# Reordering the first front and the second batch's front of an attention-plus-mixer kernel

## The chip, the core and the metric

The kernel runs on one core of a Trainium2 chip. The metric is the device time of one launch in microseconds (us), taken from several launches; the median of three runs of the kernel before is 269.89 us (269.8 to 270.16). Beside those runs there is one profiled execution of the same program, which carries a record of every instruction of the five engines: PE (TensorE, matmuls), DVE (VectorE), ACT (ScalarE), POOL (GpSimd) and SP (SyncE, which here only issues DMAs).

## The reference: what is computed

Inputs are q, k, v of shape (8 batches, 8 heads, 576 positions, 64) and four weight matrices. For each batch and head a linear attention with cosine weights is computed:

```
c, s   = cos, sin of (pi/2 * position / 576)
phi(x) = [relu(x)*c, relu(x)*s]                 64 -> 128 features
kv     = sum over positions of phi(k)^T v       128 x 64
z      = sum over positions of phi(k)           128
x      = phi(q) kv / (phi(q) z + 1e-6)          per head; heads side by side: 576 x 512
```

Then a mixer over tokens and one over channels follow, for each batch:

```
B  = relu(w_tok1^T x)          256 x 512
u  = x + w_tok2^T B            576 x 512
out = u + relu(u w_ch1) w_ch2  hidden width 1536
```

## The kernel before

A batch has 576 positions: four chunks of 128 (R = 4; chunks 0 to 3) and a tail of 64. The tails of two batches share one 128-row tile, the even batch in rows 0 to 63, the odd one in rows 64 to 127 (class `Tail`, L166). Everything that follows attention is matmul work in bf16 with results in PSUM.

Two classes carry the work of a batch. `Front` (L216) goes from q, k, v to u: `feature` (L246) makes phi of one chunk, one instruction for the cosine half and one for the sine half, on DVE or on ACT; `values` (L266) casts v; `kv` (L309) accumulates kv over the chunks, `kv_out` (L328) copies it to SBUF in two halves of four heads, half 0 on ACT and half 1 on DVE; `q_trans` (L335) transposes the eight heads of phi(q) on PE and copies them out with ACT; `num` (L353) multiplies phi(q) by kv and lets DVE divide; `tok1` (L373) and `tok1_out` (L385) make B, its first 128 rows' relu on ACT and the second 128 rows' on DVE; `tok2` (L391) makes u. `Channel` (L532) does the channel mixer: `c_main` (L540) makes one of the twelve 128-wide strips of the hidden layer (four matmuls of 512 columns, then a relu on ACT), `o_step` (L572) accumulates two of the twelve strips into a chunk of the output.

The order of the work is written out by hand, engine by engine: every engine runs its instructions in the order in which the program emits them. The main loop (L748) walks the `Channel` steps of batch b (step i makes strip i, or the next piece of the output) and after each step emits the pieces of the front of batch b+1 that `pieces` (L461) has planned for that slot. In `pieces` an entry such as `(5, KS, 2, True)` means: in slot 5, both k features of chunk 2, the sine one on ACT. QS is the same for q, QT a transpose, V a cast of v, KV the kv matmuls, N a `num`, u a `tok2` of the batch before.

Batch 0 has no earlier batch to hide behind. Its front is `first_front` (L636). It holds filler matmuls (`busy`, L202: 512-column products of the identity and zeros that nobody reads), twelve at its head and more between the pieces. It computes the denominators separately: `ksum` (L278) sums phi(k) with one-column matmuls, `ksum_out` (L291) copies the sums, `dens` (L295) multiplies phi(q) with them (eight one-column matmuls for each chunk) and `dens_out` (L305) adds 1e-6 and takes the reciprocal. The first u of batch 0 is needed transposed, as the input of the channel mixer: `turned_x` (L422) puts x transposed into four PSUM tiles (16 matmuls against the identity), `turned_b` (L430) adds the w_tok2 product to them (eight matmuls of 512 columns), and the copies at L707 write uT. The twelve matmuls of `c_block` (L552) use it at once. The u of batch 0 in its plain layout, which the output needs, is made later, in the slots of batch 1's front.

PSUM is cut into two pools of tiles: `ps_mm` (four buffers) and `ps_at` (two larger buffers). A matmul into a buffer waits until its former content has been read.

The loads: q, k, v come through SP (one through ACT). The weights w_ch1 (four DMAs, L188) and w_ch2 (L196) come through POOL, which casts them to bf16 on the way. w_ch2 is loaded in three thirds, in slot 8 of batch 1's front, on POOL's queue between two casts of v; the load of batch 2's k waits for the second third (L760). Batch 1's u is turned by DMA transposes that SP issues (`u_trans_dma`, L437) after ACT has cast u to bf16.

## Time and profile before

| what | before |
|---|---|
| median of the runs shown | 269.89 us (269.8 to 270.16) |
| time of the profiled execution | 269.69 us |
| its span, first to last instruction | 267.9 us |
| PE busy, share of the span | 261.1 us, 97% |
| DVE, ACT, POOL busy | 164.5, 129.6, 14.5 us |
| granted TensorE clock, mean | 1.000 |
| filler matmuls in the first front at L204, 512 columns | 12 at the head, 21 in all later ones |

The profiled execution is 0.20 us below the median of the runs. Its span leaves 1.79 us for what lies before the first and after the last instruction. In a timeline each row gives the start and the length of one merged group of instructions on an engine, its line, what it writes and reads and how often; a bracket at the end is the idle time of the engine just before and who ended it. Matmuls are pipelined: a row's length includes the drain of its last matmul, so the distance between the starts of neighbouring rows tells what a group took of PE's time.

### The profile page before, as it was taken

How to read it: one execution, taken by the hardware profiler on the slowest of the kernel's cores; microseconds unless marked ns; L12 is line 12 of the kernel's file. 1: busy time of each engine (PE TensorE's matmuls, PEld its weight loads, DVE VectorE, ACT ScalarE, POOL GpSimd, SP SyncE). 2: the span in 40 equal slices, each digit the busy share in tenths (PEclk: the TensorE clock that was granted, in tenths of full speed). 3: DMA queues.
4: the chain of work that ended last, by engine and by line, in shares of the span. 5: the costliest groups of instructions: out<-in, count | busy, mean ns of one | idle time of the engine just before them, and what ended most of it. 6: DMA issues, size and time to landing. Idle time of an engine off the chain costs nothing.

```text
span 267.9 us, 5123 instructions
## 1 busy us (share of the span) xinstructions
PE 261.1 (97%) x2050; PEld 139.5 (52%) x2050; DVE 164.5 (61%) x376; ACT 129.6 (48%) x228; POOL 14.5 (5%) x24
## 2 busy tenths in 40 slices
PE   7989999999999999999999999999999999999994
PEld 2665466455644455446644455446644455445543
DVE  5965798784566846876565846876565846820022
ACT  3982876428606362546516362547515362526400
POOL 6450230000000000000000000000000000000000
PEclk9999999999999999999999999999999999999999
DMA  7999999679999999469974999199974580170032
GB/s 222 359 232 270 350 175 274 225 198 290 166 340 282 273 176 346 124 166 273 209 265 117 289 223 348 59 183 239 238 253 117 157 120 0 57 200 1 2 109 87
DMA packets 91815, 53.68 MB, mean 200 GB/s; under 512 B 59408, under 2 KB 86928, under 8 KB 91792
## 3 DMA queue, kind: packets, MB, share of 16 engines
q1 hardware_dynamic: 88432, 49.62, 69.7%
q0 software_dynamic: 2832, 3.21, 7.6%
q10 hardware_dynamic: 528, 0.52, 0.6%
q8 instruction: 16, 0.26, 0.4%
q14 instruction: 7, 0.06, 0.1%
HBM read 35.85 MB, written 9.44 MB: 169 GB/s over the span
## 4 chain that ended last, share of the span: by engine, by line
PE 92%; DVE 3%; ACT 2%; DMA 2%; issue 0%; DVEq 0%; ACTq 0%
PE o_ps L579 35%; PE c_ps L546 29%; PE u_ps L406 6%; PE b_ps L382 6%; PE num_ps L359 4%; PE ct_ps L566 4%; PE kv_ps L320 3%; DMA qt<-in_q_dram 2%; DVE qp L263 1%; PE idle_ps L204 1%; PE qT_ps L340 1%; ACT v_aug L274 1%; PE c_ps L556 1%; ACT h1T L550 1%; PE t_ps L433 1%; PE d_ps L302 0%
## 5 line engine op out<-in xcount | busy, mean ns | idle before, releaser
L579 PE MATMUL o_ps<-w_ch,h1T 128*128 128x512 bf16 (+1 forms) x396 | 94.1, 372 | 0.0
L546 PE MATMUL c_ps<-uT,w_ch 128*128 128x512 bf16 (+2 forms) x384 | 92.2, 372 | 0.1
L550 ACT ACTIVATE h1T<-c_ps 128x512 bf16<-128x512 f32 x93 | 55.4, 598 | 59.9 <-PE c_ps L546 59.5
L579 PEld LDWEIGHTS <-h1T 128*128 128x128 bf16 x396 | 37.3, 98 | 39.5 <-issue 0.2
L546 PEld LDWEIGHTS <-w_ch 128*128 128x128 bf16 x384 | 33.5, 97 | 29.6 <-issue 0.2
L584 DVE TENSOR_TENSOR o_sb<-o_ps,u_sb 128x512 f32<-128x512 f32 (+1 forms) x33 | 22.3, 674 | 29.5 <-PE o_ps L579 29.4
L409 DVE TENSOR_TENSOR u_sb<-u_ps,x_sb 128x512 f32<-128x512 f32 x32 | 21.7, 689 | 6.0 <-PE u_ps L406 5.6
L413 ACT CAST u_bf<-u_sb 128x512 bf16<-128x512 f32 x28 | 17.3, 619 | 16.7 <-DVE u_sb L409 16.7
L406 PE MATMUL u_ps<-B,w_tok 128*128 128x512 bf16 x80 | 22.6, 379 | 0.0
L387 ACT ACTIVATE B<-b_ps 128x512 bf16<-128x512 f32 x8 | 4.8, 597 | 35.4 <-PE b_ps L382 35.4
L369 DVE TENSOR_TENSOR x_sb<-num_ps,den 128x512 bf16<-128x512 f32 x28 | 19.4, 692 | 1.0
L566 PEld LDWEIGHTS <-w_ch 128*128 128x128 bf16 x192 | 14.0, 98 | 9.2
L382 PE MATMUL b_ps<-x_sb,w_tok 128*128 128x512 bf16 x64 | 17.9, 379 | 0.0
L566 PE MATMUL ct_ps<-uT_tail,w_ch 128*128 128x128 bf16 x192 | 17.2, 219 | 0.0
L263 DVE TENSOR_SCALAR kp<-kt,cos_t 128x512 bf16<-128x512 f32 x32 | 15.1, 478 | 3.1 <-DMA kt<-in_k_dram 3.1
L274 ACT CAST v_aug<-vt 128x512 bf16<-128x512 f32 (+1 forms) x30 | 16.7, 586 | 0.1
L263 DVE TENSOR_SCALAR qp<-qt,cos_t 128x512 bf16<-128x512 f32 (+1 forms) x35 | 15.9, 453 | 1.0 <-DMA qt<-in_q_dram 1.0
L263 DVE TENSOR_SCALAR qp<-qt,sin_t 128x512 bf16<-128x512 f32 (+1 forms) x35 | 15.9, 453 | 0.0
L584 DVE TENSOR_TENSOR o_sb<-o_ps,u_tail 128x512 f32<-128x512 f32 x4 | 2.8, 692 | 19.0 <-PE o_ps L579 19.0
L359 PEld LDWEIGHTS <-qpT 128*128 128x128 bf16 x256 | 11.5, 98 | 5.5 <-issue 1.3
L359 PE MATMUL num_ps<-kv_sb,qpT 128*128 128x65 bf16 x256 | 13.0, 193 | 0.9 <-DVE x_sb L369 0.5
L331 DVE CAST kv_sb<-kv_ps 128x260 bf16<-128x260 f32 x8 | 3.5, 433 | 16.6 <-ACT kv_sb L331 16.5
(93 smaller groups left out, 233.4 us busy)
## 6 DMA issues: line engine op xcount, KB each, us to landing
out_dram<-o_sb SPq DMA_DIRECT2D x31, 256.0 KB, 2.9
kt<-in_k_dram SPq DMA_DIRECT2D x7, 1024.0 KB, 6.7
vt<-in_v_dram SPq DMA_DIRECT2D x7, 1024.0 KB, 6.5
qt<-in_q_dram SPq DMA_DIRECT2D x7, 1024.0 KB, 8.3
w_ch<-in_moe_w_ch_dram POOLq DMA_DIRECT2D x4, 384.0 KB, 8.3
w_ch<-in_moe_w_ch_dram POOLq DMA_DIRECT2D x3, 512.0 KB, 7.5
out_dram<-o_sb SPq DMA_DIRECT2D x10, 128.0 KB, 2.3
qtt<-in_q_dram SPq DMA_DIRECT2D x8, 128.0 KB, 5.6
```

Source lines behind the costliest of these rows:

```text
L263: nc.vector.tensor_scalar(o_ap, i_ap, scalar1=w, scalar2=0.0, op0=ALU.mult, op1=ALU.max)
L274: nc.scalar.copy(dst, src)
L359: nc.tensor.matmul(num_ps[:, g, j * DP:j * DP + D1], self.qT_of(ci, h), self.kv_sb[g][:, j, 0:D1], start=True, stop=True)
L369: nc.vector.tensor_mul(self.x_of(ci)[rows].rearrange("p (g j d) -> p g j d", g=2, j=HH), nv[:, :, :, 0:D], den.to_broadcast([rows.stop - r ...
L382: nc.tensor.matmul(self.b1_ps[mi], w, self.x_of(ci), start=(ci == ORDER[0]), stop=(ci == ORDER[-1]))
L406: nc.tensor.matmul(u_ps, w_tok2[:, ki, ci * P:(ci + 1) * P], self.B1[:, ki, :], start=(ki == 0), stop=(ki == NT - 1))
L409: nc.vector.tensor_add(u, u_ps[rows], self.x_of(ci)[rows])
L546: nc.tensor.matmul(c_ps[:, lo:hi], w_ch1[:, ki, mi * P:(mi + 1) * P], uT[:, lo // P:hi // P, ki, :], start=(ki == 0), stop=(ki == NCC - 1))
L550: nc.scalar.activation(self.h1T[:, mi, :], c_ps, AF.Relu)
L566: nc.tensor.matmul(self.ct_ps[:, mi % R, :], w_ch1[:, ki, mi * P:(mi + 1) * P], self.tail.uT[:, ki, :], start=(mi % R == 0 and ki == 0), s ...
L579: nc.tensor.matmul(o_ps, h, w_ch2[:, ki, cols], start=ki == 0, stop=ki == NCH - 1)
L584: nc.vector.tensor_add(o_sb, o_ps, u)
```

## The change

It touches the first front, the tail's transposes, the plan of batch 1's front, the order of batch 0's output steps and the load of w_ch2.

- The tail's q features are transposed by a new function, `q_trans_last`: only the batch's own 64 rows are transposed (64 columns for each head instead of 128), and ACT copies only their half of the transposed tile. The other half of that tile is set to zero once at the start by POOL, in place of half of the `qp` tail tile. It is used for batch 0 and batch 1.
- In the first front the k features are emitted first and the one-column sums behind them, with fillers of 4 (before the features) and then 2, 2, 2, 1, 0; before, there were 2, then 2 in front of each of the five sums and one behind. The v cast of chunk 0 now stands ahead of `ksum_out` on ACT and the other three behind it. All five chunks' `dens` and one `dens_out` come before the first `kv`; the two casts of w_tok1 come behind both `kv_out`s.
- Six of the sixteen `turned_x` matmuls (chunks 0 to 2 of the first two tiles) are emitted between the tail's and the last chunk's `tok1`. B's relu is made in two halves of 256 columns on each engine.
- In batch 1's front u of batch 0 is emitted in slots 4, 5, 6, 7, 8 (before: 5, 6, 8, 9, 10), the tail's v cast moves from slot 7 to 9, the q features of chunk 0 from 9 to 10, and those of chunk 2 from DVE in slot 11 to ACT in slot 10, both halves.
- w_ch2 comes in four DMAs (strips 0-1, 2-3, 4-7, 8-11) in place of three of four strips each. Batch 0's output steps alternate between chunks 0 and 1 after every two strips instead of every four. Batch 2's k waits for the third of the four DMAs, which ends with the same strip as the second third did.

```diff
@@ -177,8 +177,8 @@
             self.uT = once.tile([P, NCC, P], BF16, name="uT_tail")
     tail0 = Tail(0)
-    for t in (tail0.kp, tail0.qp):
-        nc.gpsimd.memset(t[half(1)], 0.0)
+    nc.gpsimd.memset(tail0.kp[half(1)], 0.0)
+    nc.gpsimd.memset(tail0.qpT[:, :, half(1)], 0.0)
     for g in range(2):
         nc.gpsimd.dma_start(out=w_tail1[half(g), :], in_=moe_w_tok1[SM:S, :])
     C2 = D_ch // 2
@@ -191,11 +191,10 @@
                 .rearrange("(n c) d -> c n d", c=P)))
     after(w_ch1_done[0], k_done)
     w_ch2_done = []
-    def load_w_ch2(third):
-        ki = third * NCH // 3
+    def load_w_ch2(k0, k1):
         w_ch2_done.append(nc.gpsimd.dma_start(
-            out=w_ch2[:, ki:ki + 4, :],
-            in_=moe_w_ch2[ki * P:(ki + 4) * P, :].rearrange("(n t) d -> t n d", t=P)))
+            out=w_ch2[:, k0:k1, :],
+            in_=moe_w_ch2[k0 * P:k1 * P, :].rearrange("(n t) d -> t n d", t=P)))
@@ -345,6 +344,15 @@
             else:
                 nc.vector.tensor_copy(dst, qT_ps)
+        def q_trans_last(self, pool=ps_mm):
+
+            qT_ps = pool.tile([P, H, ST], BF16, name="qT_ps", tag="mm" if pool is ps_mm else "at")
+            for h in range(H):
+                nc.tensor.transpose(qT_ps[:, h, :],
+                                    self.tail.qp[self.rows, h, :, :].rearrange("p a b -> p (a b)"),
+                                    ident[self.rows, self.rows])
+            nc.scalar.copy(self.tail.qpT[:, :, self.rows], qT_ps)
+
         def q_trans_dma(self, ci):
             dst = self.qpT[:, ci * H:(ci + 1) * H, :] if ci < R else self.tail.qpT
             nc.sync.dma_start_transpose(out=dst,
@@ -382,11 +390,11 @@
                 nc.tensor.matmul(self.b1_ps[mi], w, self.x_of(ci),
                                  start=(ci == ORDER[0]), stop=(ci == ORDER[-1]))
-        def tok1_out(self, mi, on_act=True):
+        def tok1_out(self, mi, on_act=True, cols=slice(0, Dm)):
             if on_act:
-                nc.scalar.activation(self.B1[:, mi, :], self.b1_ps[mi], AF.Relu)
-            else:
-                nc.vector.tensor_relu(self.B1[:, mi, :], self.b1_ps[mi])
+                nc.scalar.activation(self.B1[:, mi, cols], self.b1_ps[mi][:, cols], AF.Relu)
+            else:
+                nc.vector.tensor_relu(self.B1[:, mi, cols], self.b1_ps[mi][:, cols])
         def tok2(self, ci, pool=None, turn=True):
             res, tail = self.res, self.tail
@@ -419,13 +427,12 @@
             self.res["uT"] = keep.tile([P, R * NCC, P], BF16, name="uT")
-        def turned_x(self, dst, kb, first):
-
-            for ci in range(R):
+        def turned_x(self, dst, kb, chunks=range(R)):
+
+            for ci in chunks:
                 nc.tensor.matmul(dst[:, ci * P:(ci + 1) * P],
-                                 self.x[:, ci, kb * P:(kb + 1) * P], ident, start=first,
+                                 self.x[:, ci, kb * P:(kb + 1) * P], ident, start=(ci == 0),
                                  stop=False, skip_group_check=True)
-                first = False
         def turned_b(self, dst, kb, cols):
@@ -446,8 +453,8 @@
             self.feature("k", ci, 0)
             self.feature("k", ci, 1, on_act=on_act)
-        def q_side(self, ci, on_act=False):
-            self.feature("q", ci, 0)
+        def q_side(self, ci, on_act=False, both=False):
+            self.feature("q", ci, 0, on_act=both)
             self.feature("q", ci, 1, on_act=on_act)
         def mix_head(self, mi):
@@ -469,16 +476,17 @@
             if first:
                 u, act, pool = before.tok2, nc.scalar, nc.gpsimd
-                plan = [(4, KS, 0), (4, KS, 1), (5, u, 0, ps_at, False), (5, KS, 2, True),
-                        (6, KS, 3, True), (6, u, 1, ps_at, False), (7, KS, R), (7, V, R, nc.vector), (8, V, 0, act),
-                        (8, V, 2, pool), (8, load_w_ch2, 0), (8, V, 3, pool),
-                        (8, load_w_ch2, 1), (8, load_w_ch2, 2),
-                        (8, u, 2, None, False), (9, V, 1, act), (9, u, 3, None, False),
-                        (9, QS, 0), (10, u, R, None, False)]
+                plan = [(4, u, 0, ps_at, False), (4, KS, 0), (5, u, 1, ps_at, False),
+                        (5, KS, 1), (5, KS, 2, True), (6, u, 2, None, False), (6, KS, 3, True),
+                        (7, u, 3, None, False), (7, KS, R), (8, u, R, None, False),
+                        (8, V, 0, act), (8, V, 2, pool), (8, load_w_ch2, 0, 2), (8, V, 3, pool),
+                        (8, load_w_ch2, 2, 4), (8, load_w_ch2, 4, 8), (8, load_w_ch2, 8, NCH),
+                        (9, V, R, nc.vector), (9, V, 1, act),
+                        (10, QS, 0), (10, QS, 2, True, True)]
                 plan += [(11, KV, ci) for ci in range(NSC)]
-                plan += [(11, QS, 1), (11, QS, 2), (11, self.kv_out),
+                plan += [(11, QS, 1), (11, self.kv_out),
                          (11, QT, 0, (0, H), act, ps_at), (11, QT, 1), (11, QS, R),
-                         (O, QT, 2), (O, N, 0), (O, QS, 3), (O + 1, QT, R),
+                         (O, QT, 2), (O, N, 0), (O, QS, 3), (O + 1, self.q_trans_last),
                          (O + 1, N, 1), (O + 3, N, 2), (O + 3, QT, 3),
                          (O + 5, N, R), (O + 7, N, 3), (O + 8, before.tail_cast)]
             else:
@@ -616,9 +624,9 @@
             if self.b == 0:
-                for lo in range(0, NCH, 4):
+                for lo in range(0, NCH, 2):
                     for ci in (0, 1):
-                        o_range(ci, lo, lo + 4)
+                        o_range(ci, lo, lo + 2)
                 rest = (2, 3)
             elif self.b == B - 1:
                 rest = (R, 0, 1, 2)
@@ -650,37 +658,33 @@
                 f.q_trans(ci, heads)
                 busy(idle_ps, 1)
         f.q_side(R)
-        f.q_trans(R, pool=ps_at)
-        busy(idle_ps, 2)
+        f.q_trans_last(ps_at)
+        busy(idle_ps, 4)
         for ci in range(R):
             f.feature("k", ci, 0)
             f.feature("k", ci, 1, on_act=(ci > 1))
-            busy(idle_ps, 2)
+        f.k_side(R)
+        for ci in range(NSC):
+            busy(idle_ps, (2, 2, 2, 1, 0)[ci])
             f.ksum(ci)
-        f.k_side(R)
-        busy(idle_ps, 2)
-        f.ksum(R)
-        busy(idle_ps, 1)
-        for ci in range(R):
-            if ci == 2:
-                f.ksum_out()
+        f.values(0, nc.scalar, lo_heads)
+        f.ksum_out()
+        for ci in range(1, R):
             f.values(ci, nc.scalar, lo_heads)
-        cast_tok1(0)
         f.values(R, nc.vector)
         for ci in range(R):
             f.values(ci, nc.vector, hi_heads)
-        for ci in (0, 1, 2):
+        for ci in range(NSC):
             f.dens(ci)
+        f.dens_out(0, NSC * H)
         for ci in range(NSC):
             f.kv(ci, (0,))
         f.kv_out((0,))
-        for ci in (R, 3):
-            f.dens(ci)
-        f.dens_out(0, NSC * H)
         for ci in range(NSC):
             f.kv(ci, (1,))
         f.kv_out((1,))
-        cast_tok1(1)
+        for mi in range(NT):
+            cast_tok1(mi)
         for ki in range(NT):
             permute_tok2(ki)
         f.new_uT()
@@ -693,12 +697,20 @@
                 f.num(ORDER[i + 2], dens=True)
             for mi in range(NT):
                 f.tok1(mi, (ci,))
-        for mi in range(NT):
-            f.tok1_out(mi, on_act=(mi == 0))
+            if ci == R:
+
+                for kb in range(2):
+                    t_ps[kb] = ps_mm.tile([P, SM], F32, name="t_ps", tag="mm")
+                    f.turned_x(t_ps[kb], kb, range(R - 1))
+        for cols in (slice(0, DH), slice(DH, Dm)):
+            for mi in range(NT):
+                f.tok1_out(mi, on_act=(mi == 0), cols=cols)
         for kb in range(NCC):
-            t_ps[kb] = (ps_mm.tile([P, SM], F32, name="t_ps", tag="mm") if kb < 2 else
-                        ps_at.tile([P, 2, 512], F32, name="t_ps", tag="at")[:, 0, :])
-            f.turned_x(t_ps[kb], kb, first=True)
+            if kb < 2:
+                f.turned_x(t_ps[kb], kb, (R - 1,))
+                continue
+            t_ps[kb] = ps_at.tile([P, 2, 512], F32, name="t_ps", tag="at")[:, 0, :]
+            f.turned_x(t_ps[kb], kb)
         c = Channel(0, f.res, f.tail)
         by_block = f.res["uT"].rearrange("p (r k) t -> p r k t", r=R)
@@ -757,7 +769,7 @@
             if b == 0 and i == NCH:
-                load_batch(2, "kq", behind=w_ch2_done[1], tails=False)
+                load_batch(2, "kq", behind=w_ch2_done[2], tails=False)
             if b == 0 and i == NCH + 13:
                 load_batch(2, "v")
                 load_batch(2, "k", main=False)
```

## The prediction

> **What bounds the kernel now.** I read the page's busy shares and clock row first, then PE's timeline of the first front, then ACT's, PE's and DVE's where batch 1's front runs, last the landings of the DMAs that PE needs there.
>
> ```profile
> PE 261.1 (97%) x2050; PEld 139.5 (52%) x2050; DVE 164.5 (61%) x376; ACT 129.6 (48%) x228; POOL 14.5 (5%) x24
> PEclk9999999999999999999999999999999999999999
> ```
>
> PE is the bound, at full clock. Its timeline shows idle time almost only before 19 us, so whatever lets the stretch from 22 us on start sooner moves the end by as much, as long as nothing there makes PE wait.
>
> ```profile
> 10.57 0.61 PE L340 MATMUL qT_ps<-ident,qp_tail 128*128 128x128 bf16 x8 [0.17 <-DVE qp_tail L263]
> 11.01 1.03 PE L204 MATMUL idle_ps<-zeros,ident 128*128 128x512 bf16 x4
> 11.87 0.34 PE L285 MATMUL ks_ps<-ones,kp 128*128 128x1 bf16 x8
> ...
> 14.41 0.34 PE L285 MATMUL ks_ps<-ones,kp_tail 128*128 128x1 bf16 x8
> 15.00 0.74 PE L302 MATMUL d_ps<-ks_sb,qpT 128*128 128x1 bf16 x24
> 15.60 0.65 PE L320 MATMUL kv_ps<-v_aug,kp 128*128 128x65 bf16 x16
> ...
> 17.91 0.52 PE L359 MATMUL num_ps<-kv_sb,qpT 128*128 128x65 bf16 x12 [0.32 <-DVE kv_sb L331]
> 18.97 0.40 PE L359 MATMUL num_ps<-kv_sb,qpT 128*128 128x65 bf16 x8 [0.54 <-DVE x_sb L369]
> ...
> 21.50 0.59 PE L382 MATMUL b_ps<-x_sb,w_tok 128*128 128x512 bf16 x2
> 21.93 1.05 PE L425 MATMUL t_ps<-ident,x_sb 128*128 128x128 bf16 x16
> 22.82 1.89 PE L433 MATMUL t_ps<-w_tok,B 128*128 128x512 bf16 x8
> ```
>
> From 10.57 to 14.61 PE never rests: fillers (0.216 us each, four from 11.01 to 11.87) and transposes (0.056 each) set the time, not the k features. Behind the last sum comes one chain: sums out on ACT, 40 one-column matmuls (0.025 each), 40 kv matmuls (0.030 each), kv out, num, x.
>
> ```profile
> 35.97 0.60 ACT L550 ACTIVATE h1T<-c_ps 128x512 bf16<-128x512 f32 x1 [0.19 <-PE c_ps L546]
> 37.27 0.60 ACT L550 ACTIVATE h1T<-c_ps 128x512 bf16<-128x512 f32 x1 [0.70 <-PE c_ps L546]
> 38.49 0.38 ACT L331 CAST kv_sb<-kv_ps 128x260 bf16<-128x260 f32 x1 [0.62 <-PE kv_ps L320]
> 38.94 2.84 ACT L344 COPY qpT<-qT_ps 128x1024 bf16<-128x1024 bf16 x3
> ```
> ```profile
> 40.06 0.41 PE L359 MATMUL num_ps<-kv_sb,qpT 128*128 128x65 bf16 x8
> 40.30 0.59 PE L579 MATMUL o_ps<-w_ch,h1T 128*128 128x512 bf16 x2
> 40.74 0.61 PE L340 MATMUL qT_ps<-ident,qp_tail 128*128 128x128 bf16 x8
> 42.53 0.61 PE L340 MATMUL qT_ps<-ident,qp 128*128 128x128 bf16 x8
> 56.44 2.78 PE L546 MATMUL c_ps<-uT,w_ch 128*128 128x384 bf16 x24
> ```
>
> Batch 1's first num (40.06) runs just behind ACT's copy of its transposed q, which ends at 38.94 + 1.01 = 39.95: PE and ACT are level there. ACT's idle time ahead of it (0.70 and 0.62) is all the slack it has.
>
> ```profile
> DMA to landing us min/median/max: 5.9/7.5/10.1
> DMA to landing us min/median/max: 2.3/3.2/4.3
> ```
>
> The first line is w_ch2's (issued at 32.6, 34.2, 34.9, so landed at 38.5, 41.7, 45.0), the second that of the DMA transposes into uT (the one for batch 1 is issued at 52.44 and takes 3.5).
>
> **The change, part by part.**
>
> *Tail transposes and fillers.* A 64-column transpose is not in the trace; it costs at least the 0.025 of a one-column matmul and at most the 0.056 of 128 columns. I take the 65-column row, 0.030, so eight save 8 x 0.026 = 0.21 (bounds 0 to 0.25). Ahead of the last sum stand 11 fillers instead of 12: 0.22. All sums end 0.42 earlier, at 14.19. The k features stay hidden: the tail's sine ends on DVE at 13.59 and is needed at 13.98. ACT's copy of the tail halves (1.01 to about 0.5), so its two k features and the first v cast end near 13.3, before the sums. POOL's memset of the other tile is at most the 0.97 of the one removed and ends before 4 us, with nothing waiting.
>
> *Denominators in one row.* The same 80 matmuls in another order: nothing for PE. DVE's add and reciprocal (0.6) now run beside the kv matmuls, but before they ended at 17.43, when kv half 1 could be copied anyway (matmuls done at 17.22, plus 0.2 to DVE's start). Of ACT's v casts three are behind the sums; they end 1.1 us after them, at 15.45, and chunk 3 is read at about 15.9. The w_tok1 casts end at 17.8, needed at 18.8. So x of chunk 0 is just the 0.42 earlier.
>
> *Turned x and B in halves.* PE is full from 18.97 on: the tail's `tok1` ends at 21.42, 0.08 before the last chunk's. Now 21.00, plus six transposes (0.34) gives 21.34 for the last chunk's, whose x is ready at 21.08. The other ten take 21.77 to 22.32, where `turned_b` starts, against 22.82: 0.50 earlier. B's first halves (0.38 on ACT, 0.43 on DVE by the 128x260 rows of kv_sb) are ready at 22.12 and 22.39, needed at 22.32 and 22.54; whole rows on DVE (0.69) would have cost 0.11. So halving only avoids a loss.
>
> *u sooner.* The five `tok2` cost PE the same. DVE now does u of chunk 0 first, at 29.0, though batch 1's k has landed at 28.5; its queue then runs without a break to q of chunk 0 at 36.4 and chunk 1 at 37.2, needed at 37.8 and 38.2. kv needs the moved tail cast at 37.3; it ends at 36. Nothing gained or lost. But the last three strips now follow each other at 0.86 us, with no `tok2` between them.
>
> *q of chunk 2 on ACT.* This is where the gain goes. Steps on ACT: relu 0.495, v cast 0.51, q feature 0.71 (two k features of this shape from 12.12 to the next instruction at 13.54), kv out 0.275, a qpT copy 1.01. With PE 0.50 earlier and the u's out of the way, the relu of strip 9 starts at 35.06; then cast, relu, two features, relu, kv out without a pause: 35.06 + 3 x 0.495 + 0.51 + 1.42 + 0.275 = 38.75, copy done 39.76, num at 39.87 with the 0.11 that lay between them before. PE could have been there at 39.56: it waits 0.31. Of 0.50 there remain 0.19. If a feature took the full 0.80 of its row, nothing remains; if the overlap were perfect, all. I take 0.71, measured back to back. Queued behind: kv out of half 1 on DVE (0.43) starts when ACT's is done, 38.85, and is ready at 39.3, in time.
>
> *The tail's transposes of batch 1* save 0.21 on PE between that num and chunk 3's transposes (42.53). Those need q of chunk 3, which DVE makes behind x of the first num: its sine ended at 42.43, 0.11 before PE used it. DVE is 0.19 earlier, so PE is too, and the 0.21 becomes idle time. Sum still 0.19.
>
> *w_ch2 in four.* One more issue on POOL (0.75) with nothing behind it. With PE 0.2 to 0.5 earlier the strips are wanted at 38.7 (0-1), 40.5 (2-3), 42.5 (4-7) and 45.6 (8-11). Landings: below 38.5, 38.5, 41.7 and 45.0, since the queue is backlogged and the bytes are the same. Nothing. Bound: if the last issue stood behind DVE's q features (as the first w_ch1 issue did: 4.56 us instead of 0.72, until DVE's casts ended at 14.73), it would go out at 37.2 instead of 35.7, and the landing could be 1.5 later, 46.5.
> The Trainium skill, "SBUF — State Buffer", section "SBUF: two separate sides", speaks against this split: a DMA issued by GpSimd needs the port that a VectorE copy can hold for its whole length. The trace agrees at w_ch1 (4.56) and not at the first w_ch2 issue, which ran 0.77 beside the tail's k features on DVE. By the rule the sum would carry up to 0.9 us more.
>
> *Output order.* Chunk 0's output add now follows B's relu on DVE instead of leading it: B is 0.18 earlier (PE lost 0.03 on it), but the five u adds start 0.35 later, and ACT's cast and the DMA transpose with them: landing 56.0 becomes 56.34 against 56.41. Margin 0.07, no cost; the gain of 0.03 I keep.
>
> **Sum:** 0.50 - 0.31 + 0 + 0.03 = 0.22 us. The profiled run's 269.69 becomes 269.5; it lies 0.2 under the median, so 269.89 becomes 269.7.
>
> **Rivals.**
> 1. *ACT keeps up and DVE too.* PE keeps 0.50 + 0.21 + 0.03 = 0.74: 269.15. For it: PE had no idle time at all here before. Against: the sum of rows above.
> 2. *The clock drops (the other side).* From the last filler (13.8) to the first 512-column matmul (18.8) PE has 5.0 us of small matmuls with two pauses of 0.5; before, 4.4 us. The head's twelve fillers show the price: nine at 0.427 us, three at 0.216, so 3.8 us at half rate cost 1.9. Time up to 271.6; slower than 0.2% from 1.5 us at half rate on. Against: the clock row does not move with 4.4.
> The Trainium skill, "TensorE: Matmul & The Clock Gate", section "Why this matters for your kernels", asks for no PE-idle gaps over about 3 us; the pauses here are 0.5, so by it the clock stays, and the trace agrees for 4.4 us.
> 3. *uT lands late.* A transpose at the longest of its row, 4.3 instead of 3.55, turns the 0.07 into a wait of 0.68: 269.67 + 0.68 = 270.35; over 0.2% only from 0.76.
> 4. *The last quarter of w_ch2 lands at 46.5:* PE waits 0.9 from 45.6: 270.6. Against: the queue has work until 41.7, so a late issue hardly shows.
>
> **How the numbers follow.** About 0.2%, 0.54 us, is what a measurement of this kernel can tell. Forecast 0.45 (269.4 to 270.0), rival 1 0.30, rival 2 0.07, rival 3 0.10, rival 4 0.08. Faster: nearly all of rival 1 and a corner of the forecast, 0.31. Slower: rival 2, most of rival 4, a third of rival 3, and a little, 0.18. Same: 0.51. The range 269.1 to 270.4 holds the forecast, rival 3 and most of rival 1, and leaves out rivals 2 and 4.
>
> **What would show it.** `turned_b` at 22.3; ACT without a pause from 35.1 to 39.8; PE idle about 0.3 before the first num of batch 1 and 0.2 before chunk 3's transposes; no idle before uT's first use. The forecast falls if PE reaches that num below 39.6, if a slice of the clock row falls, or if a DMA ends a wait of PE.

## The result and the profile after

| what | before | after |
|---|---|---|
| median of five launches each | 269.84 us (269.71 to 270.16) | 271.16 us (270.84 to 271.55) |
| ratio | | 1.0046, interval 1.0031 to 1.0061 |
| profiled execution, its span | 269.69, 267.9 us | 271.16, 269.0 us |
| mean granted clock in it | 1.000 | 0.991 |
| PE reaches the turned B (`turned_b`) | 22.82 us | 23.33 us |
| first num of batch 1 | 40.06 us | 41.23 us |
| batch 1's first channel strip | 56.44 us | 57.59 us |

The changed kernel is 0.46% slower. I had forecast 269.7 us with a range up to 270.4, so the time lies outside it on the slow side. Of the 1.1 us that the span grew, 0.51 has been lost where PE reaches the turned B, and another 0.66 between there and the first num of batch 1; from then on the two traces run 1.15 to 1.17 apart, and 1.1 at the end. A few launches, of the kernel before too, took 556 to 1,561 us for a reason that no run shows; no ratio below contains them, and the two edits whose profiled launch was one of them (`fillers_late`, `w4_parts`) come a second time as `fillers_late2` and `w4_parts2`.

The page of the changed kernel, busy time and the row of the granted clock:

```profile
PE 262.1 (97%) x2048; PEld 140.1 (52%) x2048; DVE 164.2 (61%) x375; ACT 129.8 (48%) x231; POOL 11.2 (4%) x25
PEclk9979999999999999999999999999999999999998
```

PE is as busy as before, but one slice of the clock row fell to 7. In windows of 2 us (busy time of each engine, then the granted clock, the DMA share and GB/s):

```profile
14.00:16.00 2.00, 1.75 (x56) 1.68 (x57) 1.30 (x6) 1.08 (x4) 0.00 (x0) 0.76 1.06 356
16.00:18.00 2.00, 2.00 (x39) 1.99 (x37) 0.40 (x1) 1.10 (x3) 0.00 (x0) 0.50 1.16 248
18.00:20.00 2.00, 1.32 (x26) 1.00 (x25) 1.63 (x3) 0.47 (x2) 0.00 (x0) 0.88 1.14 206
```

The three windows add up to (0.24 + 0.50 + 0.12) x 2 us = 1.72 us of clock not granted, that is some 3.4 us at half rate. PE's timeline in that stretch:

```profile
14.56 0.97 PE L301 MATMUL d_ps<-ks_sb,qpT 128*128 128x1 bf16 x32 [0.25 <-ACT ks_sb L292]
15.60 1.04 PE L319 MATMUL kv_ps<-v_aug,kp 128*128 128x65 bf16 x16
...
23.33 1.03 PE L440 MATMUL t_ps<-w_tok,B 128*128 128x512 bf16 x4
```

The sums end 0.44 us earlier than before, as forecast (0.42), and the denominators start at 14.56 instead of 15.00. But the sixteen kv matmuls whose row took 0.65 take 1.04 here (55 ns from start to start instead of 30), and what was 0.44 early is 0.6 late at num. On ACT:

```profile
17.17 1.14 ACT L206 CAST w_tok<-u_sb 128x512 bf16<-128x512 f32 x2
19.84 1.12 ACT L209 CAST w_tok<-u_sb 128x512 bf16<-128x512 f32 x1 [1.53 <-DMA u_sb<-in_moe_w_tok_dram]
...
22.08 0.29 ACT L211 CAST w_tok<-u_sb 128x128 bf16<-128x128 f32 x1
22.75 0.66 ACT L395 ACTIVATE B<-b_ps 128x256 bf16<-128x256 f32 x2 [0.38 <-PE b_ps L390]
```

ACT waited 1.5 us for the load of w_tok2 (into the stage tile `u_sb`, L119), which landed at 19.82; before's trace had it at 16.17. Its four casts then last until 22.37, and the relu of B is queued behind them. Here PE was later still, so the wait cost nothing in this launch. Without the clock's drop it would have been next, as `first_only` below shows.

The second loss is in DVE's queue:

```profile
30.06 0.69 DVE L417 TENSOR_TENSOR u_sb<-u_ps,x_sb 128x512 f32<-128x512 f32 x1 [4.11 <-PE u_ps L414]
30.67 0.48 DVE L262 TENSOR_SCALAR kp<-kt,cos_t 128x512 bf16<-128x512 f32 x1
...
32.45 0.87 DVE L262 TENSOR_SCALAR kp<-kt,sin_t 128x512 bf16<-128x512 f32 x1
33.24 0.83 DVE L262 TENSOR_SCALAR kp<-kt,cos_t 128x512 bf16<-128x512 f32 x1
...
37.70 0.42 DVE L275 CAST v_aug<-vtt 64x512 bf16<-64x512 f32 x1
38.16 0.49 DVE L262 TENSOR_SCALAR qp<-qt,cos_t 128x512 bf16<-128x512 f32 x1
...
39.35 0.48 DVE L262 TENSOR_SCALAR qp<-qt,sin_t 128x512 bf16<-128x512 f32 x1
```

Batch 1's k had landed at 28.89, but the first k feature stands behind the first u and starts at 30.67. So the queue now hangs on PE: that u waits for PE's product until 30.06, and the 0.51 that PE has lost passes into DVE's queue. Three features take 0.8 us and more while POOL casts v and issues w_ch2 (32.4 to 36.7). q of chunk 0 starts at 38.16 and q of chunk 1 ends at 39.8. PE's side of it:

```profile
39.10 0.62 PE L339 MATMUL qT_ps<-ident,qp 128*128 128x128 bf16 x8
39.89 0.62 PE L339 MATMUL qT_ps<-ident,qp 128*128 128x128 bf16 x8 [0.17 <-DVE qp L262]
...
41.23 0.41 PE L367 MATMUL num_ps<-kv_sb,qpT 128*128 128x65 bf16 x8
...
44.14 1.03 PE L587 MATMUL o_ps<-w_ch,h1T 128*128 128x512 bf16 x4
```

Start to start, PE loses 0.17 us at 34.34 (a u tile), 0.14 at 38.93 and 0.33 at 39.50 (q of chunks 0 and 1), each time waiting for DVE. (Here and below such a time is the start of the last matmul ahead of the gap.) The row at 44.14 asks for strips 4 to 7 of w_ch2, which landed at 43.44 in this launch: no wait, but only because PE was 1.17 us late.

### The profile page after: what moved, and what is told of

The parts are those of the page before. It is cut to its first block, busy times and chain, and to the rows that moved or that the text cites. A ratio compares the mean times of both kernels' runs of the same rounds, so it can differ in the third digit from the quotient of the medians.

```text
span 269.0 us, 5122 instructions
## 1 busy us (share of the span) xinstructions
PE 262.1 (97%) x2048; PEld 140.1 (52%) x2048; DVE 164.2 (61%) x375; ACT 129.8 (48%) x231; POOL 11.2 (4%) x25
## 4 chain that ended last, share of the span: by engine, by line
PE 87%; DVE 5%; DMA 3%; ACT 2%; issue 1%; SPq 1%; DVEq 0%; ACTq 0%
PE o_ps L587 35%; PE c_ps L554 27%; PE b_ps L390 6%; PE u_ps L414 6%; PE num_ps L367 4%; PE ct_ps L574 4%; PE kv_ps L319 3%; DMA kt<-in_k_dram 3%; DVE kp L262 2%; ACT v_aug L273 1%; PE c_ps L564 1%; DVE u_sb L417 1%; ACT h1T L558 1%; DVE kp_tail L262 1%; PE t_ps L440 1%
## 5 line engine op out<-in xcount | busy, mean ns | idle before, releaser
L395 ACT ACTIVATE B<-b_ps 128x512 bf16<-128x512 f32 (+1 forms) x9 | 4.8, 549 | 33.5 <-PE b_ps L390 33.5
L330 DVE CAST kv_sb<-kv_ps 128x260 bf16<-128x260 f32 x8 | 3.5, 433 | 18.1 <-ACT kv_sb L330 16.5
```

## The experiments

Each ratio is to the kernel before, run beside it on the same chip. The times given are medians, the ratios are of means, so the two can differ a little; the intervals reach 0.10 to 0.27% to either side. "Shift" is the start of a PE row against the profiled execution of before that the prediction used. That row moves by itself: in nine profiles of kernels that have the first front of before, the turned B starts at 22.46 to 23.05, on average at 22.68 (22.82 in the prediction's). A shift of 0.3 in one launch is therefore no proof.

**The first half alone, the second half alone.** `first_only` keeps the changed first front and tail transposes and goes back to the old plan, three parts of w_ch2 and the old output order; `second_only` is its complement (both have the half-size tail transposes).

```diff
 first_only, against the changed kernel
-  plan = [(4, u, 0, ps_at, False), (4, KS, 0), (5, u, 1, ...), ... (10, QS, 0), (10, QS, 2, True, True)]
+  plan = [(4, KS, 0), (4, KS, 1), (5, u, 0, ...), ... (9, QS, 0), (10, u, R, None, False)]
-  load_w_ch2, 0, 2 / 2, 4 / 4, 8 / 8, NCH        for lo in range(0, NCH, 2)
+  load_w_ch2, 0, 4 / 4, 8 / 8, NCH               for lo in range(0, NCH, 4)
 second_only, against the changed kernel: first_front's fillers, sums, dens, casts, turned_x and relu as before
```

> The changed first front and tail transposes; batch 1's plan, w_ch2 in thirds and the output order are those of before. Theory clock (the loss is the 3.41 us at half clock): about 0.5 us slower than before, turned_b near 23.3, and later by that amount everywhere. Theory queue (the loss comes from u ahead of k on DVE in batch 1's front): without that plan PE does not wait before the second batch's transposes, so turned_b + 0.5 is all: 270.2 to 270.4 with the clock drop, and about 269.5 to 269.9 in a launch without it.

> The first front of before (with the half tail transposes), the rest as changed. Theory clock: no drop, so no loss: 269.6 to 269.9. Theory queue: the loss of batch 1's front stays, 0.4 to 0.7 us: 270.3 to 270.6, with PE waiting for q of chunks 0 and 1 from DVE at about 39. Third theory (q of chunk 2 on ACT is what delays): PE waits for ACT's copy before the first num, not for DVE.

Measured: `first_only` 269.85 us against 270.18, ratio 0.9995 (0.9977 to 1.0013). `second_only` 271.13, ratio 1.0048 (1.0025 to 1.007). The second half alone costs as much as the whole change, and the first half shows no gain. In the launch of `first_only` that was profiled the clock stayed up and num started 0.72 us early, yet the turned B came only 0.06 early. ACT and PE of `first_only`:

```profile
19.91 1.11 ACT L209 CAST w_tok<-u_sb 128x512 bf16<-128x512 f32 x1 [2.42 <-DMA u_sb<-in_moe_w_tok_dram]
...
22.34 0.63 ACT L395 ACTIVATE B<-b_ps 128x256 bf16<-128x256 f32 x2
```
```profile
22.77 1.90 PE L440 MATMUL t_ps<-w_tok,B 128*128 128x512 bf16 x8 [0.27 <-ACT B L395]
```

The load of w_tok2 landed at 19.89 and its casts ended when B's relu started. That is where 0.43 us of this launch goes. It isn't so in every launch: in `after_w3` (below), with the same first front and w_tok2 at 18.82, the casts end at 21.36 and B's relu waits for PE, yet the turned B comes at 22.57. There PE itself stood idle for 0.37 us up to 19.55, and the profile names nothing that it waited for.

**Was the early w_tok2 in before's trace the kernel's doing?** `before_again` is the kernel before, profiled once more.

> The kernel before, unchanged, once more with a profile. The question is whether its first w_ch1 issue (4.56 us, held until DVE's casts ended at 14.73) and the early landing of w_tok2 that goes with it (16.2) belong to it or to one launch. Theory load order (the short issue of 0.84 in all changed kernels comes from the change of the memset and the earlier w_tail loads): 4.5 us again, w_tok2 at 16 to 17. Theory chance (DVE happened to have no pause when k landed): 0.8 us, w_tok2 at 19 to 20, and u transposed no earlier than 22.8.

The issues of w_ch1 on POOL, first in the profile of before, then in `before_again` (minimum, median and maximum ns, first and last start):

```profile
L188 POOL DMA_DIRECT2D w_ch<-in_moe_w_ch_dram x4: 716/722/4562, 10.3 to 16.3; - x4
```
```profile
L188 POOL DMA_DIRECT2D w_ch<-in_moe_w_ch_dram x4: 791/796/840, 10.7 to 13.2; - x4
```

The same program issued its first w_ch1 load in 0.84 us this time; the three others went out at once, and w_tok2 landed at 18.89 instead of 16.17. Over the 18 profiles of launches below 272 us the first issue took 3.8 us or more in three (w_tok2 at 16.2 to 16.5); in 13 of the others it took about 0.84, with w_tok2 at 18.1 to 19.9. The remaining two are those in which w_ch1 was held (next). The prediction had built on one launch of the rarer kind.

**Let w_tok2 land first.** `first_hold` is `first_only` with the first load of w_ch1 waiting for v instead of k.

```diff
-    load_main(vt0, v, 0, HH, H)
+    v_done = load_main(vt0, v, 0, HH, H)
-    after(w_ch1_done[0], k_done)
+    after(w_ch1_done[0], v_done)
```

> The changed first front with batch 1 as before, and the first w_ch1 load held until the last v load has landed instead of the last k load. If w_tok2's late landing is what ate the gain of the first front: w_tok2 lands near 16.5 to 17, ACT's casts end before 20, turned_b starts at 22.1 to 22.4 instead of 22.77, and the time is 0.3 to 0.6 us below the changed first front without the hold. If something else ate it (the last x, the clock): no gain, or later w_ch1 landings make c_block wait.

Measured: in its profile w_tok2 lands at 15.91, the casts end at 20.0, and PE reaches the turned B at 22.10, 0.72 us early:

```profile
19.70 0.29 ACT L211 CAST w_tok<-u_sb 128x128 bf16<-128x128 f32 x1
21.53 0.66 ACT L395 ACTIVATE B<-b_ps 128x256 bf16<-128x256 f32 x2 [1.54 <-PE b_ps L390]
```

So the first front can give the 0.50 that I had worked out and more: 0.72 against the profile of before, 0.58 against the average of the nine. The time did not follow: 270.59 us against 269.71, ratio 1.0031 (1.0005 to 1.0058), with launches from 268.94, the fastest of any kernel here, to 272.4. In the profiled launch half of the lead is gone at 34.84, where PE waits 0.35 for a PSUM tile that DVE has not yet read; DVE had started on batch 1 only when k landed at 28.7. The other half is lost where PE waits for the turned tail of batch 2's q, which a DMA transpose brings:

```profile
35.41 0.59 PE L414 MATMUL u_ps<-B,w_tok 128*128 128x512 bf16 x2 [0.19 <-DVE u_sb L417]
...
73.81 0.42 PE L367 MATMUL num_ps<-kv_sb,qpT_tail 128*128 128x65 bf16 x8 [0.31 <-DMA qpT_tail<-qp_tail]
```

It landed at 73.76, and the shift goes from 0.35 early to 0.13 late. In the profile of before the same landing was at 73.60 and the use at 73.68, a margin of 0.08 that my prediction did not look at; eight of the 18 profiles lose 0.2 to 0.6 us at this place. `mix`, a second attempt, took the half-size tail transposes, the early turned x, B in halves and the hold, with the fillers, denominators, plan and w_ch2 of before:

> The kernel before with the change's half-size tail transposes, early turned x and B in halves, but the fillers, sums and denominators in the order of before, the second batch's plan and w_ch2 as before, and the first load of w_ch1 held until the last v load has landed. Theory: w_tok2 lands near 16 us, so the four weight casts do not set B; PE reaches the turned B some 0.3 to 0.5 us sooner (22.3 to 22.5) and no drop of the granted clock near 15 to 20 us; 0.2 to 0.4 us faster than the kernel before. Rival (batch 1's front is set by its own loads, k landing at 28 to 29 us, so that an earlier first batch buys nothing): turned B sooner but the first numerator of batch 1 no sooner; within 0.2 us of the kernel before.

Measured: 271.42 against 269.91, ratio 1.0047 (1.0028 to 1.0065). In its profile (its shortest launch) the turned B is 0.41 early, 0.40 is lost again at 35.15 in the same way (k landed at 29.08), and the first num of batch 1 is not earlier. That much supports the rival: batch 1's front starts when its loads land, and an earlier PE waits there. Why the median of `mix` is 1.5 us over before the one profile does not show.

**The tail transposes alone** (`tail_only`: before with `q_trans_last` and the other memset).

```diff
-        f.q_trans(R, pool=ps_at)
+        f.q_trans_last(ps_at)
-                         ... (O, QS, 3), (O + 1, QT, R),
+                         ... (O, QS, 3), (O + 1, self.q_trans_last),
```

> Before with the half tail transposes and the other memset alone. Theory load order: the first w_ch1 issue takes 0.84 us, w_tok2 lands at 19 to 20, ACT's four casts of w_tok2 end at 21.5 to 22.4 and turned_b starts 0 to 0.2 us later than before although PE has 0.2 us less to do: 0 to +0.2 us. Theory chance: no fixed sign, within 0.1 us of before.

Measured: 270.25 against 269.71, ratio 1.0014 (0.9996 to 1.0033): no gain.

**The clock.** `fillers_late` is the changed kernel with fourteen fillers in place of eleven, set later in the run of sums; `fillers_late2` is the same edit again.

```diff
         for ci in range(NSC):
-            busy(idle_ps, (2, 2, 2, 1, 0)[ci])
+            busy(idle_ps, (0, 2, 2, 2, 2)[ci])
             f.ksum(ci)
+        busy(idle_ps, 2)
```

> As changed, but with the fillers moved towards the end of the sums and two behind them (4, then 0, 2, 2, 2, 2, then 2). Theory clock: the granted clock stays at 1.0, turned_b comes back from 23.3 to 22.4 or 22.6, and the time falls by 0.7 to 0.9 us to about 270.3. Theory queue: turned_b comes back too, but u of chunk 0 still stands ahead of k on DVE, so a wait for DVE before the transposes of q is left and the time stays 0.3 us or more above before. If the clock drops all the same, the number of fillers is not what decides.

> The same edit as fillers_late (three fillers of 512 columns more, set later in the run of sums, denominators and values of batch 0), for a usable profile. Theory: the granted clock stays at 1.0 through 15 to 20 us in every launch, the products of batch 0's kv run at 30 ns instead of 50, turned B still near 22.8 to 23.3 us because the fillers (0.65 us) and the late second part of the token weights take what the clock gives; the front of batch 1 late by 0.5 to 0.7 us as in the changed kernel, so 0.3 to 0.6% slower than before. Rival (the clock was the loss): within 0.2% of the kernel before.

Measured: 271.63 (ratio 1.0053, 1.003 to 1.0076) and 271.43 (1.0054, 1.0036 to 1.0072). The mean clock was 0.999 or 1.000 in the eleven launches that count, against 0.991 to 0.993 in three of five of the changed kernel. The windows of `fillers_late2`:

```profile
14.00:16.00 2.00, 2.00 (x58) 1.64 (x57) 0.89 (x5) 1.08 (x4) 2.00 (x4) 1.00 1.05 352
16.00:18.00 2.00, 1.70 (x55) 1.60 (x51) 1.03 (x3) 1.38 (x4) 0.21 (x1) 1.00 1.14 201
```

So the drop can be taken away, and the time does not come back. (The three added fillers cost PE 0.216 each, 0.65 us, themselves.) In this launch the turned B was 0.26 early and the first num of batch 1 0.05 early. Then PE stopped:

```profile
44.54 1.02 PE L587 MATMUL o_ps<-w_ch,h1T 128*128 128x512 bf16 x3 [1.32 <-DMA w_ch<-in_moe_w_ch_dram]
```

The part of w_ch2 with strips 4 to 7 landed at 44.50. Start to start PE lost 1.49 us, and batch 1's first strip was 1.53 late. My own theory of this run (batch 1's front 0.5 to 0.7 late) missed the place, and the rival (the clock was the whole loss) fell.

**Which piece of the second half?** Five kernels, each the kernel before with one piece.

```diff
 u_only      -(5, u, 0) (6, u, 1) (8, u, 2) (9, u, 3) (10, u, R)   +(4, u, 0) (5, u, 1) (6, u, 2) (7, u, 3) (8, u, R)
 qs2_act     -(7, V, R) (9, QS, 0) (11, QS, 2)                     +(9, V, R) (10, QS, 0) (10, QS, 2, True, True)
 plan_only   both of these, w_ch2 in three parts, old output order
 w4_order    -load_w_ch2 in thirds, range(0, NCH, 4)               +0:2, 2:4, 4:8, 8:NCH and range(0, NCH, 2)
 order_only  -range(0, NCH, 4)                                     +range(0, NCH, 2)
```

> Before with the five u of batch 0 in the new slots 4 to 8 and nothing else. Theory queue (u of chunk 0 holds DVE's queue until 29.5, while k of batch 1 is there from 28.5, and everything behind it on DVE is a microsecond late): 0.3 to 0.8 us slower than before, with PE waiting at kv or at the first transposes for DVE's k and q features. ACT theory (q of chunk 2 on ACT is what costs): no change, within 0.1 us.

> The kernel before with nothing of the change but the second batch's plan: the five adds of u first, v of the tail in slot 9, q of chunk 0 in slot 10, q of chunk 2 on ScalarE in slot 10; w_ch2 in three parts and the output order as before. Theory (the queue of VectorE): the whole cost of the second half of the change sits here, because the k features start behind u and the q features of chunks 0 and 1 come after v of the tail; first sum of batch 1 0.5 to 0.9 us late, 0.4 to 0.8 us over the kernel before in the median (some 270.2 to 270.6 beside 269.8). Rival (the cost comes from w_ch2 in four parts and the output order): no more than 0.2 us over the kernel before, as the move of u alone was (0.06%).

> The kernel before with u where it was, and only q of chunk 2 moved to ScalarE (slot 10), with v of the tail in slot 9 and q of chunk 0 in slot 10 as in the changed kernel. Theory (queue of VectorE, u first and q late both needed): VectorE has u behind k as before and two features fewer, so q of chunks 0 and 1 are in time; ScalarE's 1.5 us of q features delay the copies of the turned q by 0.3 us; 0 to 0.3 us over the kernel before. Rival (the move of the q features alone is the cost): 0.4 us or more over it, with the first numerator product waiting for q of chunk 0 or for ScalarE's copy.

> The kernel before with only w_ch2 in four parts and batch 0's output by two strips at a time. Theory: nothing in the batch-1 front moves; within 0.2 us of the kernel before, perhaps 0.1 to 0.3 us faster where a launch has the last third of w_ch2 late (a wait of 0.5 us at 45.7 us in one trace of the kernel before). Rival (the four parts collide with the q loads and the cost of the change's second half is here): 0.4 us or more slower.

> The kernel before with w_ch2 in three parts as before and only batch 0's first output in steps of two strips. Theory (the parts are the cost): within 0.15% of the kernel before, since strips 4 to 7 are asked for after the same eight steps. Rival (the output order itself costs): 0.3 to 0.5% slower, as with parts and order together.

| kernel | median, before's | ratio, interval |
|---|---|---|
| u_only | 270.01, 269.71 | 1.0006, 0.9991 to 1.002 |
| qs2_act | 270.26, 269.91 | 1.0019, 1.0005 to 1.0032 |
| plan_only | 270.38, 269.91 | 1.0022, 1.0007 to 1.0037 |
| w4_order | 271.0, 269.91 | 1.0048, 1.0029 to 1.0067 |
| order_only | 270.0, 269.79 | 1.0007, 0.9994 to 1.002 |

The plan costs 0.22%, about what I expected; w_ch2 with the output order costs 0.48%, which I had expected to be nothing; the output order alone cannot be told from no change. Within the plan my theory of DVE's queue missed: I had expected 0.3 to 0.8 us from u first alone, and `u_only` cannot be told from no change either, although DVE is late in its profile:

```profile
29.34 0.69 DVE L409 TENSOR_TENSOR u_sb<-u_ps,x_sb 128x512 f32<-128x512 f32 x1 [4.11 <-PE c_ps L545]
29.95 0.48 DVE L263 TENSOR_SCALAR kp<-kt,cos_t 128x512 bf16<-128x512 f32 x1
...
36.98 0.47 DVE L263 TENSOR_SCALAR qp<-qt,cos_t 128x512 bf16<-128x512 f32 x1
```

q of chunk 0 starts at 36.98 instead of 35.74, but PE waits for DVE only 0.13 on the way to the first num, at a u tile. The moved q features alone (`qs2_act`) measured 0.19%, nearly as much as the whole plan; the intervals do not say how the two share its cost. `w4_order` on PE:

```profile
43.67 1.02 PE L578 MATMUL o_ps<-w_ch,h1T 128*128 128x512 bf16 x3 [0.39 <-DMA w_ch<-in_moe_w_ch_dram]
```

PE is level with before up to the first num (shift -0.03) and then loses 0.55, start to start, for strips 4 to 7, which land at 43.63, and 0.18 at 40.49, waiting for DVE. Batch 2's k, which waits for the same part, lands at 51.06 instead of 47.76, and at 74.15 PE waits 0.38 for batch 2's turned tail, as in `first_hold`. Three parts are not free of this either. `order_only` waits for strips 4 to 7 (and loses 0.24 at 38.84 for its first part, which landed at 39.10), `before_again` for its third part (strips 8 to 11):

```profile
43.29 1.02 PE L579 MATMUL o_ps<-w_ch,h1T 128*128 128x512 bf16 x4 [0.17 <-DMA w_ch<-in_moe_w_ch_dram]
```
```profile
46.39 0.59 PE L579 MATMUL o_ps<-w_ch,h1T 128*128 128x512 bf16 x2 [0.35 <-DMA w_ch<-in_moe_w_ch_dram]
```

In `qs2_act`'s profile (its longest launch, span 269.4, all loads late: q at 36.75) PE loses 0.56 at 39.6, ahead of batch 0's first output step. The profile puts it to ACT's copy of the turned q:

```profile
40.21 0.39 PE L579 MATMUL o_ps<-w_ch,h1T 128*128 128x512 bf16 x1 [0.40 <-ACT qpT L344]
```

But the same matmul of the kernel before does not need that copy. It ran in the middle of it (38.94 to 39.95):

```profile
39.18 0.59 PE L579 MATMUL o_ps<-w_ch,h1T 128*128 128x512 bf16 x2
```

It also waits for strips 0 to 3 of w_ch2, and in `qs2_act` they landed at 40.16. So this wait too was most likely for a load. The wait that the prediction had priced at 0.31 can be seen in `fillers_late2`, where ACT runs without a pause from 36.28 to the end of its copy at 39.95 and the first num starts right behind it, 0.11 late:

```profile
38.66 0.38 ACT L330 CAST kv_sb<-kv_ps 128x260 bf16<-128x260 f32 x1
38.92 2.86 ACT L343 COPY qpT<-qT_ps 128x1024 bf16<-128x1024 bf16 x3
```
```profile
40.01 0.42 PE L367 MATMUL num_ps<-kv_sb,qpT 128*128 128x65 bf16 x8
```

**The parts alone, and earlier.** `w4_parts` (run again as `w4_parts2`) is before with w_ch2 in four parts and the old output order; `w_ahead` is before with the second third issued ahead of POOL's cast of v of chunk 3.

```diff
 w4_parts
-  (8, V, 2, pool), (8, load_w_ch2, 0), (8, V, 3, pool), (8, load_w_ch2, 1), (8, load_w_ch2, 2),
+  (8, V, 2, pool), (8, load_w_ch2, 0, 2), (8, V, 3, pool), (8, load_w_ch2, 2, 4), (8, load_w_ch2, 4, 8), (8, load_w_ch2, 8, NCH),
 w_ahead
-  (8, V, 2, pool), (8, load_w_ch2, 0), (8, V, 3, pool), (8, load_w_ch2, 1), (8, load_w_ch2, 2),
+  (8, V, 2, pool), (8, load_w_ch2, 0), (8, load_w_ch2, 1), (8, V, 3, pool), (8, load_w_ch2, 2),
```

> The kernel before with only w_ch2 in four parts (2, 2, 4 and 4 strips); the output order as before. Theory: the part with strips 4 to 7 is issued one DMA later on GpSimd (0.75 us) and lands near 43.2 us instead of 42.4, when PE asks for it at 43.0; the loads of batch 2 wait for it too; 0.3 to 0.5% slower. Also the second part (strips 2 and 3) is asked for two steps sooner than with the order in twos, at 39.6 to 40.3 us, and lands near 40: one more wait of up to 0.5 us. Rival (the output order is the cost): within 0.15%.

> The same edit as w4_parts, for a usable profile. Theory: PE waits for a part of w_ch2 within batch 0's first output (at 39 to 41 us for strips 2 and 3, or at 43 to 44 us for strips 4 to 7), 0.3 to 0.7 us in all, and batch 2's k and q land 1 to 3 us later than with three parts; 0.2 to 0.5% slower than before. Rival: no wait for w_ch2 on PE and the loss elsewhere.

> The kernel before with the second third of w_ch2 (strips 4 to 7) issued ahead of the cast of v of chunk 3 on GpSimd instead of behind it, some 0.8 us sooner. Theory (the time of issue sets the landing): the second third lands near 41.7 us instead of 42.4 and the third lands as before; 0 to 0.2% faster than the kernel before in the median. Rival (the landings are set by the pace of the 16 queues, which are never empty from 21 to 46 us): landings and time the same; or the cast of v of chunk 3, now 0.8 us later on GpSimd, delays kv of batch 1 and it is 0.1 to 0.3% slower.

Measured: `w4_parts` 270.77 against 269.79, ratio 1.0034 (1.0018 to 1.0051); again, 270.08 against 269.71, ratio 1.0017 (1.0002 to 1.0032). So the parts carry the cost of that pair, though not always as much. The second run's profile came from one of its shorter launches (269.56): the part landed at 42.82 and PE lost 0.11. How late strips 4 to 7 are can be read from all profiles, counted from the landing of batch 1's q just ahead of them: 6.4 to 7.5 us later with three parts (twelve profiles, mean 7.08), 7.3 to 8.3 with four (six profiles, mean 7.88). PE asks for them at about 43.0 if it is not late. Landings were 41.3 to 44.1 with three parts and 42.6 to 44.5 with four: the split moves a landing that was level with its use by 0.8 us.

`w_ahead` was 269.56 against 269.79, ratio 0.9999 (0.9988 to 1.001), no different. The second third went out at 32.90 instead of 34.18 and landed at 42.26, 7.4 after q: an earlier issue does not bring an earlier landing. That speaks for the pace of the queues against the time of issue; why the same bytes then take 0.8 us longer in four parts stays open.

**How the pieces share the loss inside the changed kernel.** `u_late` is the changed kernel with u in its old slots; `after_w3` is the changed kernel with three parts of w_ch2 and the old output order.

```diff
 u_late   -(4, u, 0) (5, u, 1) (6, u, 2) (7, u, 3) (8, u, R)       +(5, u, 0) (6, u, 1) (8, u, 2) (9, u, 3) (10, u, R)
 after_w3 -0:2, 2:4, 4:8, 8:NCH and range(0, NCH, 2)               +0:4, 4:8, 8:NCH and range(0, NCH, 4)
```

> As changed, but u of batch 0 in the slots of before (5, 6, 8, 9, 10), k first. Theory clock: nothing changes, 271.0 to 271.3. Theory queue: DVE starts on batch 1's k when it lands (about 28.9) and is ahead of PE again; the waits before the transposes of q (0.17 and 0.33) and before the last u (0.17) go, so 0.5 to 0.65 us less: about 270.5. ACT theory: the time stays, since q of chunk 2 is still on ACT.

> The changed kernel with w_ch2 in three parts and the output order of before, all else as changed. Theory (the plan of VectorE, w_ch2's parts and the clock each cost a part, and their waits overlap): 0.1 to 0.3% faster than the changed kernel, that is 0.15 to 0.35% slower than the kernel before. Rival (w_ch2's parts were the whole loss): within 0.15% of the kernel before. Other rival (with the first sum of batch 1 late by 1.2 us, w_ch2 is never waited for): no different from the changed kernel, 0.45% slower than before.

Measured: `u_late` 270.46 against 270.18, ratio 1.0027 (1.0003 to 1.0051); `after_w3` 270.57 against 269.79, ratio 1.0026 (1.0011 to 1.0042). Each gives back some 0.2 of the 0.46%, which fits the pieces (0.22% for the plan, 0.17 and 0.34% for the parts), but the intervals reach to that of the changed kernel. `u_late` shows what u first had done; DVE in its profile:

```profile
28.41 0.49 DVE L262 TENSOR_SCALAR kp<-kt,cos_t 128x512 bf16<-128x512 f32 x1 [2.81 <-DMA kt<-in_k_dram]
...
35.98 0.42 DVE L275 CAST v_aug<-vtt 64x512 bf16<-64x512 f32 x1
36.44 0.49 DVE L262 TENSOR_SCALAR qp<-qt,cos_t 128x512 bf16<-128x512 f32 x1
```

DVE starts on k the moment it lands, and reaches q of chunk 0 at 36.44 instead of 38.16. From the turned B to the first num of batch 1 the shift stays at +0.15. With u first it grew in all five such profiles with the full plan: by 0.30 (`plan_only`), 0.33 (`second_only`), 0.43 (`after_w3`), 0.21 (`fillers_late2`) and 0.66 (the changed kernel). That growth alone is no proof: `plan_only` has 0.12 of it from strips 0 to 3 of w_ch2 and `fillers_late2` half of it from ACT's copy, and where PE was early it grew without u first as well (0.25 in `order_only`, 0.35 in `first_hold`, 0.46 in `mix`). In the changed kernel and in `second_only`, where PE was late already, nearly all of it is waits for DVE.

No version was faster than the kernel before beyond its interval.

## Why the prediction was wrong, step by step

The step that failed most clearly is "*w_ch2 in four: Nothing*": the split cost 0.17 and 0.34% alone. The plan of batch 1's front, put at nothing but the 0.31 on ACT, cost 0.22%. Against that stood the 0.50 of the first front, which did not show in the time (`first_only`, 0.9995, though its interval still allows it). How these pieces add up to the 0.46% of the changed kernel is not settled.

- *Tail transposes and fillers:* right. The sums ended 0.44 early (0.42 forecast). The eight 64-column transposes took 0.33 instead of the 0.24 that I took, 0.09 of it a pause.
- *Denominators in one row, "x of chunk 0 is just the 0.42 earlier":* wrong in the changed kernel's own launch, where the clock fell. The other order of the same 80 matmuls was not free: a drop (a mean clock of 0.991 to 0.994) came in 12 of 47 launches of the five kernels with the changed first front and its fillers (the changed kernel, `first_only`, `u_late`, `first_hold`, `after_w3`), and in none of 126 timed launches of the kernel before, nor in the eleven with fillers late. This is rival 2, to which I gave 0.07. Its condition as I put it, 5.0 us of small matmuls, does not decide: 35 of the 47 launches ran the same 5.0 us and kept the clock, and the drop at 15.06 came 1.7 us after the last filler. Its price was too high: within the changed kernel the launches with a drop have spans of 269.0 to 269.4, those without 268.7. `first_only` and `after_w3` show about the same 0.5, while in `first_hold` and `u_late` the launches with a drop are no longer than the others. So it is a part of the loss, some 0.5 us in three of five launches, and the kernel is slower without it as well.
  The Trainium skill, "TensorE: Matmul & The Clock Gate", section "Why this matters for your kernels", asks for no idle gaps over about 3 us. The trace differs, for the clock fell without one: PE's longest pause from 10.8 us to the drop at 15.06 was 0.4 us, start to start. The Trainium skill, "TensorE: Matmul & The Clock Gate", section "What's actually happening", has a free-running window of 3413 ns; the stretch at half rate lasted 3.41 us here and came in some launches only, which agrees.
- *"w_tok1 casts end at 17.8, needed at 18.8":* true but not the limit. I left out the four w_tok2 casts behind them in ACT's queue, and the load that they wait for. The step *turned x and B in halves* (22.32) fails by it in `first_only` (22.77), and holds where w_tok2 was let in first (22.10). Even then the 0.50 does not reach the end: PE meets a u tile that DVE has not read, and the turned tail of batch 2 (`first_hold`).
- *"u sooner: nothing gained or lost":* right for u alone (`u_only`, 1.0006), wrong in the changed kernel's own launch. I had DVE's queue reach q of chunk 0 at 36.4, with features at their short length. In the changed kernel it was 38.16, in `fillers_late2` 36.8 and in `u_only` 37.0. The first k feature waits behind u, three features run at about double length beside POOL's casts and issues, and with u first a late PE makes DVE late too. PE lost 0.64 us to DVE in that launch, 0.1 to 0.4 in the other four with the full plan.
- *q of chunk 2 on ACT, 0.31 on PE:* the mechanism exists, at 0.11 in `fillers_late2`. In the changed kernel PE waited for DVE's q instead, so this price came with the one above and not beside it.
- *"w_ch2 in four: Nothing":* mis-sized. It measured 0.17 and 0.34% alone, and PE waits for strips 4 to 7 in three of the six profiles with four parts (0.11, 0.55 and 1.49 us). In the changed kernel's own profile it does not, because it came late. I had used the landings of one launch (41.7 for strips 4 to 7, needed at 42.5), which is early among twelve (41.3 to 44.1). Rival 4 looked at the last part; the late one is the third. The Trainium skill's rule on GpSimd's DMA issues and VectorE's port ("SBUF — State Buffer", section "SBUF: two separate sides"), which spoke against this split, is not what decided: no issue of a part of w_ch2 took over 1.0 us in any profile here.
- *The tail's transposes of batch 1 and the output order:* right in that neither moves the end (1.0014 and 1.0007, both intervals across 1). The landing of batch 1's uT came 0.05 before its use; I had forecast 0.07.
- *The rivals as a set:* I gave one chance to each as if they excluded one another. The plan, the parts and the clock are three costs at neighbouring places, which hide each other in part, as the row at 44.14 shows: PE was late enough not to meet a late load. All of them point to the slow side, while the forecast's 0.50 had a single condition: that everything else on the path be ready as early. It was not.

## What to carry to other kernels

Where PE and the loads are level, work taken from PE buys nothing until the loads come sooner: look for the next landing that PE will meet, and for its spread over several launches, since the single trace of before had two of them (w_tok2 and strips 4 to 7 of w_ch2) among the earliest seen later, and a third (batch 2's turned tail) only 0.08 us before its use. On an engine with a full queue, an instruction put ahead of one whose data has already landed delays all that follows; what that costs in time depends on who waits at the end (nothing measurable in `u_only`). And fillers are part of the clock: reordering small matmuls around them needs a look at the clock of many launches, not of one.

## What the runs showed that I had not expected

- The granted clock fell to 0.50 for 3.41 us although PE never paused longer than 0.4 us in the 4 us ahead. Ahead of it stood the same 11 fillers as in launches that kept the clock; with 14, placed later, it stayed up in eleven of eleven. In both profiled launches with a drop (the changed kernel and `u_late`) it began 10.2 us, three times 3.41, after the head's fillers had quickened from 0.427 to 0.216 us (near 4.8 and 6.0). `first_only` quickened near 4.8 as well and kept the clock. That the placing relative to a fixed window decides is my reading; it was not tested apart from the number.
- The first issue of w_ch1 on POOL took 4.56 us in one launch of the kernel before and 0.84 in the next profiled one, and w_tok2's landing moved from 16.17 to 18.89 with it.
- A DVE feature takes 0.40 us start to start, and 0.75 to 0.79 beside POOL's first cast of v, first issue of w_ch2 and second cast (the rows at 32.45 and 33.24 above).
- Launches of one kernel at full clock spread by more than the effects: `mix` from 268.2 to 270.3 in span. What differs in the slow ones the profiles, one for each kernel, do not show; it stays open.
